# One decode step of attention and a gated feed-forward layer: q as four rows, one loop for heads 0 to 30, and the two projections summed in one row

## The chip, the cores and the metric

The kernel runs on one core of a Trainium2 chip. The metric is the device time of one execution in microseconds (us). Before the change it was 2518.3 us (median of four runs, 2518.19 to 2518.62). The names of the engines are those of the profile: PE multiplies matrices, PEld is its weight load, DVE and ACT are the vector and the scalar engine, SP issues nearly all DMA transfers.

## The reference, cut to what matters

One query token attends to a cache of 65536 positions in each of 32 heads, beside a small feed-forward layer; a gate mixes the two.

```python
# D = 512, H = 32, Sk = 65536, Dh = 128, F = 1792; all bfloat16
g = sigmoid((x * gate_w).sum(-1))
q = (x @ wq).reshape(H, Dh)
p = softmax(q @ k_cache[h].T * Dh ** -0.5)     # per head
a = concat_h(p @ v_cache[h]) @ wo
b = (silu(x @ w_gate) * (x @ w_up)) @ w_down
out = g * a + (1 - g) * b
```

k and v are 2 x 32 x 65536 x 128 x 2 bytes = 1073.7 MB. Everything else is 14 MB. Each byte is used once.

## The kernel before

Each head is cut into two chunks of 32768 positions, so there are 64 chunks. A chunk's k is one transfer of 8.39 MB and its v is another. They go in turn through a ring of three slots in SBUF, all on SP's queue. SP waits before it issues a transfer until the slot that it writes is free.

```python
WQ = KT * H * Dh
wq_sb = view(0, 0, KT, H * Dh)
dma("wq", wq_sb, ...)                            # 4.2 MB, slot 0
load("k", 0, [EK] * (KPP // EK))                 # slot 1, four pieces of 64 rows
dma("gate", gate_v, ...); dma("up", up_v, ...)   # 3.7 MB, rest of slot 0
load("v", 0, [KPP])                              # slot 2

# q as a column for each head: 32 x 4 matmuls of one column, each with its own weights
group("q_ps", [(m_x[:, h : h + 1],
    [(wq_sb[:, t, h * Dh : (h + 1) * Dh], Xc[:, t : t + 1]) for t in range(KT)])
    for h in range(H)], ...)
act("qT", qT, m_x[:, :H], ACT.Copy, ["m_x"], ["qT"])

def spread(h):                                   # q of one head into all partitions
    act("dq", dq, ident, ACT.Copy, ["ident", "qT"], ["dq"], scale=qT[:, h : h + 1])
    mms("spread", m_sp[:, :Dh], [(ones_b, dq)], ["ones_b", "dq"], ["m_sp"])
    act("q_bc", q_bc[q], m_sp[:, :Dh], ACT.Copy, ["m_sp"], [("q_bc", q)])
...
def block(n, j, m):       # DVE multiplies k by q in place; PE sums the products
...                       # gather(): DVE reduces the sums, ACT takes exp
def pv(n):                # 64 matmuls of 4 x 512: the weights times v
...
spread(0)
for n in range(N - 1):
    ...
    if n: load("k", n, [KPP]); load("v", n, [KPP])
    m = EK if n in (0, N - 2) else HK
    for j in range(0, KPP, m):
        block(n, j, m)
        ...
    gather()
    if n == 0:
        gate(); hidden()                         # frees slot 0
    ...
```

PE's instructions of heads 1 to 30 are a loop of ten turns of three heads; head 0 and head 31 are written out. In the last chunk PE also does both projections, and the last v comes in five pieces (128, 64, 32, 16 and 16 rows), so that little work is left behind the last one:

```python
row("b_ps", wd, ...)                     # m_x[0:1] = h @ w_down
act("row_b", row_b, m_x[0:1, :D], ..., scale=ngval[0:1, :])
row("a_ps", wo, ...)                     # m_sp[0:1] = o @ wo without the last head
act("row_a", row_a, m_sp[0:1, :D], ..., scale=gval[0:1, :])
for i, j in enumerate(range(0, KPP, EK)):
    if i == 2:                           # turn both rows to 4 x 128, eight matmuls in fp32
        mms("rest_ps", m_sp[:OT, :P], [... for r in (row_b, row_a) for q in range(OT)], ...)
        act("rest4", ...)
    block(n, j, EK)
    ...
column(n, V_END[:1]); sum_ps(h, H); norm(h, H); column(n, V_END[1:], V_END[0])
# then Z, l_ps, out_sb and the output's transfer
```

The softmax here doesn't subtract the row's maximum and nothing guards it: scores larger than these inputs give would overflow.

## Time and profile before

| What | Value | Read from |
|---|---|---|
| time; span of the profiled run | 2518.3 us; 2516.7 us | runs; page |
| bytes moved by DMA | 1088.04 MB | page, part 2 |
| DMA rate, 320 to 2440 us | 434 GB/s | DMA view of that window |
| first transfer issued | 1.0 us | timeline |
| last piece of v usable, output issued | 2512.1, 2514.2 us | timeline |

The lines of the page that say what bounds the kernel are the DMA rows. The first line of the fence gives busy time and share of the span of two engines; the rows after it are shares and GB/s in 40 equal slices; then comes the data queue with packets, MB and share of the 16 DMA engines' span, the queue of instruction packets, and the chain of work that ended last, by engine.

```profile
PE 1972.7 (78%) x9177; PEld 410.3 (16%) x5215; DVE 1268.4 (50%) x291; ACT 99.2 (4%) x404; POOL 1.9 (0%) x9
...
DMA  9999999999999999999999999999999999999998
GB/s 423 432 433 433 433 432 437 434 435 434 433 433 433 434 437 433 434 433 433 433 433 434 434 432 435 435 435 435 434 433 433 433 434 436 434 433 434 433 434 376
...
q1 hardware_dynamic: 20744, 1087.78, 99.8%
q8 instruction: 13, 0.21, 0.0%
...
DMA 46%; PE 40%; DVE 13%; ACT 1%; issue 0%; another core or an unknown queue 0%; SPq 0%; DVEq 0%; ACTq 0%
```

The rate is 432 to 437 GB/s in all but the first and the last slice, and 434 in the mean from 320 to 2440 us. The Trainium skill, "DMA: Bandwidth & Descriptors", section "Where 436 GB/s comes from", gives 435.2 GB/s as the ceiling of the path into SBUF, so this trace sits on it. The last line would suggest that PE is 40% of the problem. It says only that each transfer was *issued* when PE had freed its slot; it doesn't say that the queue had run out of work by then. That must be read from issue times, as in the timeline of the start. Columns: start, us, engine, line, operation, output and input, count, and idle time of the engine with what ended it.

```profile
13.21 3.57 PE L285 MATMUL m_x<-Xc,slot_65 128*128 128x1 bf16 x128 [10.62 <-DMA slot_65<-in_A_wq_dram]
18.29 4.42 DVE L344 TENSOR_TENSOR slot_66<-slot_66,q_bc_78 128x8192 bf16<-128x8192 bf16 x1 [15.50 <-ACT q_bc_78 L294]
45.11 6.86 PE L285 MATMUL m_x<-Xc,slot_65 128*128 128x1 bf16 x112 [0.35 <-ACT gval L294]
51.99 0.33 SPq L181 DMA_DIRECT2D slot_65<-in_A_k_cache_dram  x1
52.37 0.43 SPq L181 DMA_DIRECT2D slot_66<-in_A_v_cache_dram  x1
61.77 16.18 PE L257 MATMUL O_ps<-slot_67,P_sb_83 128*4 128x512 bf16 x64 [9.80 <-DMA slot_67<-in_A_v_cache_dram]
77.98 0.33 SPq L181 DMA_DIRECT2D slot_67<-in_A_k_cache_dram  x1
```

The PV matmuls of chunk 0 start when v has landed (61.8 us). By then k and v of chunk 1 have been in the queue for nearly 10 us. A transfer of 8.39 MB takes 19.3 us at this rate, so k of chunk 1 lands near 81 us and v near 100 us, and k of chunk 2 is issued at 78.0 us. The queue is never empty.

The timeline of the end shows the other edge of the stream. The first two lines are the last exp of the last chunk (ACT), the next four are PE's work on the last v.

```profile
2501.66 0.26 ACT L294 ACTIVATE P_sb_84<-S_sb_82 128x64 bf16<-128x64 f32 x1 [3.46 <-DVE S_sb_82 L369]
2501.82 0.19 ACT L294 ACTIVATION_READ_ACCUMULATOR P_sb_84<-S_sb_82 128x1 f32 x1
2502.09 3.44 PE L257 MATMUL m_c<-P_sb_84,slot_65 128*128 128x1 bf16 x127 [1.20 <-ACT P_sb_84 L294]
2508.09 0.18 PE L257 MATMUL m_c<-P_sb_84,slot_65 128*128 128x1 bf16 x1 [2.56 <-issue]
2508.56 3.12 PE L257 MATMUL m_c<-P_sb_84,slot_65 128*128 128x1 bf16 x112
2512.12 0.77 PE L257 MATMUL m_c<-P_sb_84,slot_65 128*128 128x1 bf16 x16 [0.43 <-DMA slot_65<-in_A_v_cache_dram]
...
2514.20 0.34 SPq L181 DMA_DIRECT2D out_dram<-out_sb  x1
```

PE waits at the end for the last piece of v (2512.12), and the output's transfer is issued 2.1 us later.

### The profile page before, as it was taken

The numbers are of one execution on the slowest core, as the hardware profiler recorded it, in microseconds if no ns is written. First come the engines' busy times: TensorE is split into PE (matmuls) and PEld (weight loads), VectorE is DVE, ScalarE is ACT, GpSimd is POOL, SyncE is SP. The second block draws the span as 40 slices with busy tenths as digits, with TensorE's granted clock in tenths as the row PEclk, the third lists the DMA queues.
The fourth block names the chain that finished last, engine by engine and source line by source line (L and its number), as shares of the span: only waits on it lengthen the run. The fifth ranks groups of instructions, "written<-read, shape, count | busy, mean of one in ns | idle before, by whom it ended". The sixth has DMA issues, their size and how long they took to land.

```text
span 2516.7 us, 15579 instructions
## 1 busy us (share of the span) xinstructions
PE 1972.7 (78%) x9177; PEld 410.3 (16%) x5215; DVE 1268.4 (50%) x291; ACT 99.2 (4%) x404; POOL 1.9 (0%) x9
## 2 busy tenths in 40 slices
PE   4777877877878778778787787787877877877787
PEld 1111111111111111111111111111111111111113
DVE  3455355464553554644545546446455364464554
ACT  0000000000000000000000000000000000000000
POOL 0000000000000000000000000000000000000000
PEclk8899989989889889899898899898988989989898
DMA  9999999999999999999999999999999999999998
GB/s 423 432 433 433 433 432 437 434 435 434 433 433 433 434 437 433 434 433 433 433 433 434 434 432 435 435 435 435 434 433 433 433 434 436 434 433 434 433 434 376
DMA packets 20767, 1088.04 MB, mean 432 GB/s; under 512 B 2314, under 2 KB 2444, under 8 KB 2700
## 3 DMA queue, kind: packets, MB, share of 16 engines
q1 hardware_dynamic: 20744, 1087.78, 99.8%
q8 instruction: 13, 0.21, 0.0%
q14 instruction: 6, 0.05, 0.0%
q10 hardware_dynamic: 4, 0.00, 0.0%
HBM read 1087.77 MB, written 0.00 MB: 432 GB/s over the span
## 4 chain that ended last, share of the span: by engine, by line
DMA 46%; PE 40%; DVE 13%; ACT 1%; issue 0%; another core or an unknown queue 0%; SPq 0%; DVEq 0%; ACTq 0%
PE O_ps L257 17%; DMA slot_67<-in_A_k_cache_dram 16%; DMA slot_65<-in_A_k_cache_dram 14%; DMA slot_66<-in_A_k_cache_dram 14%; PE S_ps_103 L275 11%; PE S_ps_104 L275 8%; DVE slot_66 L344 4%; DVE slot_67 L344 4%; DVE slot_65 L344 3%; DMA slot_65<-in_A_v_cache_dram 2%; DVE S_sb_82 L369 2%; PE m_c L257 1%; PE S_ps_103 L285 1%; ACT P_sb_83 L294 0%; DMA slot_65<-in_A_wq_dram 0%
## 5 line engine op out<-in xcount | busy, mean ns | idle before, releaser
L344 DVE TENSOR_TENSOR slot_67<-slot_67,q_bc_79 128x16384 bf16<-128x16384 bf16 (+1 forms) x28 | 208.2, 7469 | 146.5 <-DMA slot_67<-in_A_k_cache_dram 146.5
L369 DVE TENSOR_REDUCE S_sb_82<-S_ps_104 128x128 f32<-128x1024 f32 (+1 forms) x67 | 78.8, 1177 | 392.0 <-PE S_ps_104 L275 392.0
L344 DVE TENSOR_TENSOR slot_65<-slot_65,q_bc_78 128x16384 bf16<-128x16384 bf16 x22 | 190.2, 8689 | 146.3 <-DMA slot_65<-in_A_k_cache_dram 146.3
L344 DVE TENSOR_TENSOR slot_66<-slot_66,q_bc_78 128x16384 bf16<-128x16384 bf16 (+1 forms) x24 | 190.6, 7978 | 138.0 <-DMA slot_66<-in_A_k_cache_dram 122.5
L344 DVE TENSOR_TENSOR slot_66<-slot_66,q_bc_79 128x16384 bf16<-128x16384 bf16 x20 | 172.9, 8689 | 122.4 <-DMA slot_66<-in_A_k_cache_dram 122.4
L344 DVE TENSOR_TENSOR slot_65<-slot_65,q_bc_79 128x16384 bf16<-128x16384 bf16 x20 | 172.9, 8689 | 120.2 <-DMA slot_65<-in_A_k_cache_dram 120.2
L344 DVE TENSOR_TENSOR slot_67<-slot_67,q_bc_78 128x16384 bf16<-128x16384 bf16 x20 | 172.9, 8689 | 117.8 <-DMA slot_67<-in_A_k_cache_dram 117.8
L275 PE MATMUL S_ps_103<-slot_65,ident 128*128 128x512 bf16 x651 | 186.6, 457 | 0.0
L275 PE MATMUL S_ps_103<-slot_67,ident 128*128 128x512 bf16 x680 | 185.8, 441 | 0.0
L275 PE MATMUL S_ps_103<-slot_66,ident 128*128 128x512 bf16 x650 | 184.9, 454 | 0.0
L257 PE MATMUL O_ps<-slot_67,P_sb_83 128*4 128x512 bf16 x704 | 155.9, 383 | 28.1 <-ACT P_sb_83 L294 18.3
L257 PE MATMUL O_ps<-slot_66,P_sb_84 128*4 128x512 bf16 x704 | 153.7, 379 | 19.3 <-ACT P_sb_84 L294 19.3
L257 PE MATMUL O_ps<-slot_65,P_sb_83 128*4 128x512 bf16 x640 | 139.7, 379 | 18.3 <-ACT P_sb_83 L294 18.3
L257 PE MATMUL O_ps<-slot_67,P_sb_84 128*4 128x512 bf16 x640 | 139.7, 379 | 18.3 <-ACT P_sb_84 L294 18.3
L257 PE MATMUL O_ps<-slot_65,P_sb_84 128*4 128x512 bf16 x640 | 139.7, 379 | 18.3 <-ACT P_sb_84 L294 18.3
L257 PE MATMUL O_ps<-slot_66,P_sb_83 128*4 128x512 bf16 x640 | 139.8, 379 | 17.5 <-ACT P_sb_83 L294 17.5
L275 PE MATMUL S_ps_104<-slot_67,ident 128*128 128x512 bf16 x680 | 150.7, 379 | 0.0
L275 PE MATMUL S_ps_104<-slot_65,ident 128*128 128x512 bf16 x651 | 143.9, 379 | 0.0
L275 PE MATMUL S_ps_104<-slot_66,ident 128*128 128x512 bf16 x650 | 143.9, 379 | 0.0
L285 PE MATMUL S_ps_103<-slot_65,ident 128*128 128x512 bf16 x21 | 12.8, 608 | 134.9 <-DVE slot_65 L344 134.9
L285 PE MATMUL S_ps_103<-slot_66,ident 128*128 128x512 bf16 x22 | 13.2, 598 | 134.2 <-DVE slot_66 L344 134.2
L285 PE MATMUL S_ps_103<-slot_67,ident 128*128 128x512 bf16 x24 | 13.9, 581 | 125.0 <-DVE slot_67 L344 125.0
(99 smaller groups left out, 719.0 us busy)
## 6 DMA issues: line engine op xcount, KB each, us to landing
slot_66<-in_A_k_cache_dram SPq DMA_DIRECT2D x4, 2048.0 KB, 24.4
slot_67<-in_A_k_cache_dram SPq DMA_DIRECT2D x4, 2048.0 KB, 30.7
slot_65<-in_A_wq_dram SPq DMA_DIRECT2D x1, 4096.0 KB, 12.1
slot_66<-in_A_wo_dram SPq DMA_DIRECT2D x1, 4096.0 KB, 32.5
slot_65<-in_A_v_cache_dram SPq DMA_DIRECT2D x1, 4096.0 KB, 37.4
slot_65<-in_A_v_cache_dram SPq DMA_DIRECT2D x1, 2048.0 KB, 40.7
slot_65<-in_B_w_gate_dram SPq DMA_DIRECT2D x1, 1792.0 KB, 34.6
slot_65<-in_B_w_up_dram SPq DMA_DIRECT2D x1, 1792.0 KB, 38.3
```

The source lines that it names most:

```text
L257: ins = nc.tensor.matmul(out_ap, lhsT=a, rhs=b, start=start and i == 0, stop=stop and i == len(pairs) - 1,)
L275: ins = nc.tensor.add_instruction(mybir.InstMatmult(name=nc.get_next_instruction_name(), engine=mybir.EngineType.PE, ins=[nc.tensor.lower_ ...
L285: ins = nc.tensor.matmul(out_ap, lhsT=a, rhs=b, start=first, stop=last)
L344: "products", lambda: nc.vector.tensor_tensor(out=w, in0=w, in1=q_rep, op=ALU.mult),
L369: lambda: nc.vector.tensor_reduce(out=S_sb[b][:, :m], in_=S_ps[r][:, :m, :], axis=AXIS.X, op=ALU.add),
```

## The change

It is meant to make PE's program shorter and the constants smaller:

- q becomes four rows of 1024 (partitions 0, 32, 64 and 96), with a column of x as the stationary operand of two matmuls of 512 columns at a time: 16 weight loads and 32 matmuls instead of 128 of each. The spread of one head then contracts over one row.
- gate and up are loaded ahead of k of chunk 0, and the gate and the hidden layer are computed ahead of it. So head 0 is like the others, and PE's loop runs over heads 0 to 30: eleven turns of three heads, with an exit after the first head of the last turn.
- The two projections are summed in one row: ACT writes (1-g)*b, DVE adds g*a. Turning the row takes four fp32 matmuls instead of eight, one block later.

The diff, cut to its core:

```diff
-    load("k", 0, [EK] * (KPP // EK))
     ... gate, up ...
+    load("k", 0, [HK] * (KPP // HK))
     load("v", 0, [KPP])
@@ q
-            (m_x[:, h : h + 1],
-             [(wq_sb[:, t, h * Dh : (h + 1) * Dh], Xc[:, t : t + 1]) for t in range(KT)])
-            for h in range(H)
+            [(q_ps[32 * g : 32 * g + 1, i * W : (i + 1) * W],
+              [(x_col, wq_sb[:, t, (2 * g + i) * W : (2 * g + i + 1) * W])
+               for t, x_col in enumerate(x_cols)])
+             for i in range(2)]
+            ... for g in range(OT)
-    act("qT", qT, m_x[:, :H], ACT.Copy, ["m_x"], ["qT"])
+    for g in range(OT):
+        act("q4", q4[32 * g : 32 * g + 1, :], q_ps[32 * g : 32 * g + 1, :], ACT.Copy, ...)
@@ spread
-        act("dq", dq, ident, ACT.Copy, ["ident", "qT"], ["dq"], scale=qT[:, h : h + 1])
-        mms("spread", m_sp[:, :Dh], [(ones_b, dq)], ["ones_b", "dq"], ["m_sp"])
+        act("dq", dq, q4[32 * g : 32 * g + 1, i * Dh : (i + 1) * Dh], ACT.Copy, ...)
+        mms("spread", m_sp[:, :Dh], [(ones_b[0:1, :], dq)], ["ones_b", "dq"], ["m_sp"])
@@ start
+    gate()
+    hidden()
+    act("O_sb0", O_sb, ones[0:VB, 0:1].to_broadcast([VB, VB * Dh]), ACT.Copy, ["ones"], ["O_sb"])
     spread(0)
-        m = EK if n in (0, N - 2) else HK
+        m = EK if n == N - 2 else HK
-        if n == 0:
-            gate()
-            hidden()
@@ tail
-    row_a = O_sb[0:1, :D]
-    act("row_a", row_a, m_sp[0:1, :D], ACT.Copy, ..., scale=gval[0:1, :])
-        if i == 2:   # rest_ps: eight matmuls over (row_b, row_a)
+        if i == 3:   # rest_ps: four matmuls over row
+        if i == 1:
+            dve("row2", lambda: nc.vector.scalar_tensor_tensor(
+                out=row[:, :D], in0=m_sp[0:1, :D], scalar=gval[0:1, :], in1=row[:, :D],
+                op0=ALU.mult, op1=ALU.add), ...)
@@ PE's program
-        with nc.Fori(0, rounds, 1, engines=[PE], head_slot={PE: 0}) as r:
-            for i, o in enumerate(body[0]):
-                put(o, {s: val + r * step[i, s] for s, val in o.waits.items()})
+        with nc.Fori(0, rounds + 1, 1, engines=[PE], head_slot={PE: 0}) as r:
+            turn_of(0, r)
+            with nc.tensor.If(r < rounds):
+                for i in range(1, BODY):
+                    turn_of(i, r)
```

More of the change, by code (lines that the diff above doesn't have):

```diff
@@ L122 @@
     slot = [ring_pool.tile([P, SLOT], bf16, name=f"slot{i}") for i in range(SLOTS)]
-    x_row = sb("x_row", [1, D], bf16)
-    gw_row = sb("gw_row", [1, D], bf16)
+    row = sb("row", [1, 3 * D // 2], f32)
+    x_row, gw_row, xg = (row.bitcast(bf16)[:, i * D : (i + 1) * D] for i in range(3))
     ones = sb("ones", [P, P], f32)
@@ L130 @@
     Xc = sb("Xc", [P, KT], bf16)
-    qT = sb("qT", [P, H], f32)
-    dq = sb("dq", [P, Dh], bf16)
+    QP = H // OT
+    q4 = sb("q4", [P, QP * Dh], bf16)
+    dq = sb("dq", [1, Dh], bf16)
     q_bc = [sb(f"q_bc{i}", [P, Dh], bf16) for i in range(2)]
@@ L144 @@
     eg = sb("eg", [P, FT], f32)
-    xg = sb("xg", [1, D], bf16)
     s_t = sb("s_t", [1, 1], f32)
@@ L148 @@
     rest4 = sb("rest4", [OT, P], f32)
-    row_b = sb("row_b", [1, D], f32)
     unit = sb("unit", [1, OT * OT], f32)
@@ L269, in fn @@
             held = None
-            for out_ap, pairs in parts:
-                for i, (a, b) in enumerate(pairs):
-                    first, last = i == 0, i == len(pairs) - 1
-                    if a is held:
-                        ins = nc.tensor.add_instruction(
-                            mybir.InstMatmult(
-                                name=nc.get_next_instruction_name(), engine=mybir.EngineType.PE,
-                                ins=[nc.tensor.lower_ap(b), weights],
-                                outs=[nc.tensor.lower_ap(out_ap)],
-                                start_tensor_calc=first, stop_tensor_calc=last,
-                                tile_size=(P, P), tile_position=(0, 0), ldweights=False,
-                            )
-                        )
-                    else:
-                        ins = nc.tensor.matmul(out_ap, lhsT=a, rhs=b, start=first, stop=last)
-                        weights = ins.ins.ins[1]
-                    held = a
+            for part in parts:
+                part = part if isinstance(part, list) else [part]
+                for i in range(len(part[0][1])):
+                    for out_ap, pairs in part:
+                        a, b = pairs[i]
+                        first, last = i == 0, i == len(pairs) - 1
+                        if a is held:
+                            ins = nc.tensor.add_instruction(
+                                mybir.InstMatmult(
+                                    name=nc.get_next_instruction_name(),
+                                    engine=mybir.EngineType.PE,
+                                    ins=[nc.tensor.lower_ap(b), load.ins[1]],
+                                    outs=[nc.tensor.lower_ap(out_ap)],
+                                    start_tensor_calc=first, stop_tensor_calc=last,
+                                    tile_size=load.tile_size, tile_position=load.tile_position,
+                                    ldweights=False,
+                                )
+                            )
+                        else:
+                            ins = nc.tensor.matmul(out_ap, lhsT=a, rhs=b, start=first, stop=last)
+                            load = ins.ins
+                        held = a
             return ins
@@ L310 @@
     dve("Xc", lambda: nc.vector.tensor_copy(out=Xc, in_=m_x[:, :KT]), ["m_x"], ["Xc"])
+    q_ps = S_ps[0].rearrange("p k r -> p (k r)")
+    W = 512
+    assert QP * Dh == 2 * W
     group(
@@ L315 @@
         [
-            (
-                m_x[:, h : h + 1],
-                [(wq_sb[:, t, h * Dh : (h + 1) * Dh], Xc[:, t : t + 1]) for t in range(KT)],
-            )
-            for h in range(H)
+            [
+                (
+                    q_ps[32 * g : 32 * g + 1, i * W : (i + 1) * W],
+                    [
+                        (x_col, wq_sb[:, t, (2 * g + i) * W : (2 * g + i + 1) * W])
+                        for t, x_col in enumerate(x_cols)
+                    ],
+                )
+                for i in range(2)
+            ]
+            for x_cols in [[Xc[:, t : t + 1] for t in range(KT)]]
+            for g in range(OT)
         ],
-        units(0, 0, WQ) + ["Xc"], ["m_x"],
+        units(0, 0, WQ) + ["Xc"], [("S_ps", 0)],
     )
-    act("qT", qT, m_x[:, :H], ACT.Copy, ["m_x"], ["qT"])
+    for g in range(OT):
+        act("q4", q4[32 * g : 32 * g + 1, :], q_ps[32 * g : 32 * g + 1, :], ACT.Copy,
+            [("S_ps", 0)], [("q4", g)])
     def spread(h):
-        act("dq", dq, ident, ACT.Copy, ["ident", "qT"], ["dq"], scale=qT[:, h : h + 1])
-        mms("spread", m_sp[:, :Dh], [(ones_b, dq)], ["ones_b", "dq"], ["m_sp"])
+        g, i = divmod(h, QP)
+        act("dq", dq, q4[32 * g : 32 * g + 1, i * Dh : (i + 1) * Dh], ACT.Copy,
+            [("q4", g)], ["dq"])
+        mms("spread", m_sp[:, :Dh], [(ones_b[0:1, :], dq)], ["ones_b", "dq"], ["m_sp"])
         q = h % 2
@@ L382 @@
     P_all = [("P_sb", i, u) for i in range(2) for u in range(RS)]
-    pending = []
+    pending = [H - 1]
     def pv(n):
@@ L474, in gate, with project @@
         )
-    def row(key, w_v, names, cols, cname, ks, bank, bname):
+    EARLY = ["x_row", "gw_row", "xg"]
+    def project(key, w_v, names, cols, cname, ks, bank, bname):
         mms(key, bank[0:1, :D], [(cols[:, k : k + 1], w_v[:, k, :]) for k in ks],
@@ L570 @@
     turn_outputs(1)
-    row("b_ps", wd, units(ws, 0, WO), hT, "hT", range(FT), m_x, "m_x")
-    act("row_b", row_b, m_x[0:1, :D], ACT.Copy, ["m_x", "ngval"], ["row_b"], scale=ngval[0:1, :])
-    row("a_ps", wo, units(ws, WO, WL), M, "M", range(H), m_sp, "m_sp")
-    row_a = O_sb[0:1, :D]
-    act("row_a", row_a, m_sp[0:1, :D], ACT.Copy, ["m_sp", "gval"], ["O_sb"], scale=gval[0:1, :])
+    project("b_ps", wd, units(ws, 0, WO), hT, "hT", range(FT), m_x, "m_x")
+    act("row", row[:, :D], m_x[0:1, :D], ACT.Copy, ["m_x", "ngval"], ["row"] + EARLY,
+        scale=ngval[0:1, :])
+    project("a_ps", wo, units(ws, WO, WL), M, "M", range(H), m_sp, "m_sp")
     for i, j in enumerate(range(0, KPP, EK)):
-        if i == 2:
+        if i == 3:
             mms(
@@ L581 @@
                 [
-                    (unit[:, OT * q : OT * (q + 1)], r[:, P * q : P * (q + 1)])
-                    for r in (row_b, row_a)
+                    (unit[:, OT * q : OT * (q + 1)], row[:, P * q : P * (q + 1)])
                     for q in range(OT)
                 ],
-                ["unit", "O_sb", "row_b"], ["m_sp"],
+                ["unit", "row"], ["m_sp"],
             )
@@ L589 @@
         block(n, j, EK)
+        if i == 1:
+            dve(
+                "row2",
+                lambda: nc.vector.scalar_tensor_tensor(
+                    out=row[:, :D], in0=m_sp[0:1, :D], scalar=gval[0:1, :], in1=row[:, :D],
+                    op0=ALU.mult, op1=ALU.add,
+                ),
+                ["m_sp", "gval", "row"], ["row"],
+            )
         while len(todo) > 1:
@@ L622 @@
     rounds = (H - 2) // BODY
-    first, last = 1, 1 + rounds * BODY
+    assert H == 2 + rounds * BODY
     with tc.tile_critical():
@@ L643, in pe @@
         def pe(a, b):
-            return [o for o in plan.ops[cut[a] if a else 0 : b] if o.engine == "PE"]
-        for o in pe(0, cut[first]):
+            return [o for o in plan.ops[a:b] if o.engine == "PE"]
+        for o in pe(0, cut[0]):
             put(o, o.waits)
-        body = [pe(first + r * BODY, cut[first + (r + 1) * BODY]) for r in range(rounds)]
+        heads = [pe(cut[h], cut[h + 1]) for h in range(H - 1)]
+        body = [[heads[r * BODY + i] for i in range(BODY)] for r in range(rounds)]
@@ L649 @@
+        body.append([heads[rounds * BODY]])
         step = {}
-        for i, o in enumerate(body[0]):
-            if "POOL" in o.waits:
-                nc.tensor.wait_ge(sems["POOL"], o.waits.pop("POOL"))
-            for s, val in o.waits.items():
-                step[i, s] = body[1][i].waits[s] - val if rounds > 1 else 0
-            for r, b in enumerate(body):
-                assert b[i].key == o.key, (b[i].key, o.key)
-                assert b[i].waits == {
-                    s: val + r * step[i, s] for s, val in o.waits.items()
-                }, (r, o.key, o.waits, b[i].waits)
@@ L660 @@
-        PE = mybir.EngineType.PE
-        with nc.Fori(0, rounds, 1, engines=[PE], head_slot={PE: 0}) as r:
-            for i, o in enumerate(body[0]):
-                put(o, {s: val + r * step[i, s] for s, val in o.waits.items()})
-        for o in pe(last, len(plan.ops)):
+        for i in range(BODY):
+            for j, o in enumerate(body[0][i]):
+                if "POOL" in o.waits:
+                    nc.tensor.wait_ge(sems["POOL"], o.waits.pop("POOL"))
+                for s, val in o.waits.items():
+                    step[i, j, s] = body[1][i][j].waits[s] - val
+                for r, b in enumerate(body):
+                    if i < len(b):
+                        assert b[i][j].key == o.key, (b[i][j].key, o.key)
+                        assert b[i][j].waits == {
+                            s: val + r * step[i, j, s] for s, val in o.waits.items()
+                        }, (r, o.key, o.waits, b[i][j].waits)
@@ L665, with turn_of @@
+        def turn_of(i, r):
+            for j, o in enumerate(body[0][i]):
+                put(o, {s: val + r * step[i, j, s] for s, val in o.waits.items()})
+        PE = mybir.EngineType.PE
+        with nc.Fori(0, rounds + 1, 1, engines=[PE], head_slot={PE: 0}) as r:
[3 more added lines that the diff above has]
+                    turn_of(i, r)
+        for o in pe(cut[H - 1], len(plan.ops)):
             put(o, o.waits)
```

## The prediction

> **What bounds the kernel.** Its DMA queue. The page gives 1088 MB over 2516.7 us, the data queue busy 99.8%; between 320 and 2440 us every slice shows 432 to 435 GB/s. The Trainium skill, "DMA: Bandwidth & Descriptors", section "Where 436 GB/s comes from", puts the fabric's ceiling at 435.2 GB/s; this trace sits on it. PE (78%) and DVE (50%) have slack. The SP view of waits and the timeline show each load issued well before its turn: k of chunk 1 at 52 us, though the queue is full until v of chunk 0 lands at 61.8; later about a whole transfer (19.3 us) is still queued. Only the bytes, the work before the first transfer (1.0 us) and after the last landing (2512.1 us to the output issue at 2514.2) can move the time.
>
> **What the change does.** It changes no bytes.
>
> 1. Start. q was 128 weight loads and 128 one-column matmuls, 3.6 us (timeline, 13.2 to 16.8). Now 32 matmuls of 512 columns: at the 0.41 us (slow clock) and 0.22 us (full clock) spacing that the trace shows for this shape, 7 to 10 us, estimated. Then four ACT copies of 1x1024, some 1.2 us each (estimate from 0.68 us for 1x512). Gate and hidden now come first (PE 3 to 7 us), so the first product on DVE starts at 31 to 35 us instead of 18.3. Head 0's first half of k lands near 31.4 us, the second near 41, v at 60 to 61.5 (estimated from bytes and rate), so the PV matmuls still start near 61 us, as before at 61.8. Slot 0 is freed at 27 to 33 us instead of 52, slot 1 at about 57 instead of 52; the queue needs them at 61 and 81. Off the path. Two DMAs fewer may save 0.2 to 0.4 us [...].
>
> 2. Each head: dq is one row and the spread matmul contracts over one row; ACT is cheaper by 0.2 to 0.3 us. Off the path. The branch adds tenths of us of PE time per turn, against some 8 us of PE slack per chunk. Instruction packets: none on queue 8 between 320 and 2440 us, so the loop is not refetched; "Runtime: NRT & Kernel Launch", section "Instruction fetch mechanics", gives PE 2048 instructions; the body, about 1220, still fits.
>
> 3. Tail. The scaled a-row moves from ACT to DVE (512 elements, about 0.65 us), behind the second product, where DVE is the bound (products and reductions back to back from 2482 to 2497). It delays the last exp from 2501.7 to about 2502.3. Eight fp32 matmuls become four, where PE has slack. The column matmuls (3.4 us, an idle of 2.6 us beside an instruction packet, 3.1 us) end at 2511.7, and the last piece of v lands at 2512.1. So 0 to 0.5 us shows.
>
> **Predicted:** 2518.2 us, 8 in 10 within 2517.0 to 2519.6. Faster by over 2%: 0.005; within 2%: 0.985; slower: 0.01.
>
> **What would show it.** Right: 433 to 435 GB/s in every middle slice, first product at 31 to 35 us, PV of chunk 0 near 61, k of chunk 1 issued near 30, last v landing within 1 us of 2512. The last exp about 0.6 us later relative to the last k landing.
>
> **What would make it wrong.** A loop with an inner exit that is refetched each turn (packets on queue 8 in the middle, PE idle by "issue"); q later than estimated, so that PV of chunk 0 slips beyond 75 us and the queue runs dry; the instruction-fetch idle in the last columns falling elsewhere (up to 2.5 us either way).

## The result, and the profile after

The changed kernel took 2518.59 us (median of four fast runs, 2518.18 to 2519.18), the kernel before 2518.28 us beside it. The ratio is 1.0001, with a 95% interval of 0.9984 to 1.0018: the same.

The same lines of the page, of the changed kernel:

```profile
PE 1977.6 (79%) x9081; PEld 405.9 (16%) x5101; DVE 1268.6 (50%) x288; ACT 101.9 (4%) x404; POOL 1.9 (0%) x9
...
GB/s 423 433 433 432 432 434 433 433 434 438 434 433 433 433 433 433 435 436 435 434 434 433 433 433 433 434 433 434 438 434 433 434 433 433 433 434 435 435 434 377
...
q1 hardware_dynamic: 20456, 1087.78, 99.8%
q8 instruction: 11, 0.18, 0.0%
...
DMA 47%; PE 39%; DVE 13%; ACT 0%; issue 0%; another core or an unknown queue 0%; SPq 0%
```

The bytes of the data queue are the same, 1087.78 MB, and so is the rate. Two instruction packets are gone. The start has been rearranged, as its timeline shows:

```profile
13.42 0.58 PE L290 MATMUL S_ps_100<-slot_65,Xc 128*1 128x512 bf16 x1 [10.84 <-DMA slot_65<-in_A_wq_dram]
...
19.77 4.13 ACT L299 ACTIVATE q_75<-S_ps_100 1x1024 bf16<-1x1024 f32 x4 [16.71 <-PE S_ps_100 L278]
24.24 6.85 PE L290 MATMUL m_x<-Xc,slot_65 128*128 128x1 bf16 x112 [4.20 <-ACT gval L299]
31.12 0.33 SPq L181 DMA_DIRECT2D slot_65<-in_A_k_cache_dram  x1
33.07 8.69 DVE L363 TENSOR_TENSOR slot_66<-slot_66,q_bc_77 128x16384 bf16<-128x16384 bf16 x1 [0.60 <-DMA slot_66<-in_A_k_cache_dram]
58.94 0.33 SPq L181 DMA_DIRECT2D slot_66<-in_A_v_cache_dram  x1
61.91 15.66 PE L257 MATMUL O_ps<-slot_67,P_sb_82 128*4 128x512 bf16 x64 [2.99 <-DMA slot_67<-in_A_v_cache_dram]
77.60 0.33 SPq L181 DMA_DIRECT2D slot_67<-in_A_k_cache_dram  x1
```

The first product is 14.8 us later (33.07 against 18.29). k of chunk 1 is issued 20.9 us earlier, v of chunk 1 is issued 6.6 us later, and none of it matters: the PV matmuls of chunk 0 wait for the landing of v and start at 61.9 us, 0.1 us from where they were. At the end:

```profile
2487.38 0.73 DVE L613 SCALAR_TENSOR_TENSOR row<-m_sp,gval,row 1x512 f32<-1x512 f32 x1
...
2502.42 0.26 ACT L299 ACTIVATE P_sb_83<-S_sb_81 128x64 bf16<-128x64 f32 x1 [3.46 <-DVE S_sb_81 L388]
2502.50 3.34 PE L257 MATMUL m_c<-P_sb_83,slot_65 128*128 128x1 bf16 x128 [0.84 <-DMA slot_65<-in_A_v_cache_dram]
2508.44 3.06 PE L257 MATMUL m_c<-P_sb_83,slot_65 128*128 128x1 bf16 x108 [0.92 <-issue]
2512.14 0.59 PE L257 MATMUL m_c<-P_sb_83,slot_65 128*128 128x1 bf16 x16 [0.64 <-DMA slot_65<-in_A_v_cache_dram]
...
2514.04 0.34 SPq L181 DMA_DIRECT2D out_dram<-out_sb  x1
```

The new DVE operation took 0.73 us, and the last exp came 0.76 us later than before. PE again waits for the last piece of v, at 2512.14 against 2512.12 us.

### The profile page after: what moved, and what is told of

It reads as the page before. It is cut to its first block, busy times and chain, and to the rows that moved or that the text cites. A ratio compares the mean times of both kernels' runs of the same rounds, so it can differ in the third digit from the quotient of the medians.

```text
span 2516.5 us, 15383 instructions
## 1 busy us (share of the span) xinstructions
PE 1977.6 (79%) x9081; PEld 405.9 (16%) x5101; DVE 1268.6 (50%) x288; ACT 101.9 (4%) x404; POOL 1.9 (0%) x9
## 3 DMA queue, kind: packets, MB, share of 16 engines
q1 hardware_dynamic: 20456, 1087.78, 99.8%
## 4 chain that ended last, share of the span: by engine, by line
DMA 47%; PE 39%; DVE 13%; ACT 0%; issue 0%; another core or an unknown queue 0%; SPq 0%
PE O_ps L257 17%; DMA slot_67<-in_A_k_cache_dram 16%; DMA slot_66<-in_A_k_cache_dram 15%; DMA slot_65<-in_A_k_cache_dram 14%; PE S_ps_100 L278 11%; PE S_ps_101 L278 9%; DVE slot_67 L363 4%; DVE slot_66 L363 4%; DVE slot_65 L363 3%; DMA slot_65<-in_A_v_cache_dram 2%; DVE S_sb_81 L388 1%; PE m_c L257 1%; PE S_ps_100 L290 1%; ACT P_sb_82 L299 0%; PE S_ps_101 L290 0%
## 5 line engine op out<-in xcount | busy, mean ns | idle before, releaser
L363 DVE TENSOR_TENSOR slot_67<-slot_67,q_bc_78 128x16384 bf16<-128x16384 bf16 (+1 forms) x28 | 208.2, 7467 | 143.8 <-DMA slot_67<-in_A_k_cache_dram 143.8
L363 DVE TENSOR_TENSOR slot_65<-slot_65,q_bc_77 128x16384 bf16<-128x16384 bf16 x22 | 190.2, 8688 | 140.2 <-DMA slot_65<-in_A_k_cache_dram 140.2
L363 DVE TENSOR_TENSOR slot_66<-slot_66,q_bc_77 128x16384 bf16<-128x16384 bf16 x22 | 190.3, 8688 | 122.9 <-DMA slot_66<-in_A_k_cache_dram 122.9
L363 DVE TENSOR_TENSOR slot_65<-slot_65,q_bc_78 128x16384 bf16<-128x16384 bf16 x20 | 172.9, 8688 | 120.7 <-DMA slot_65<-in_A_k_cache_dram 120.7
L363 DVE TENSOR_TENSOR slot_66<-slot_66,q_bc_78 128x16384 bf16<-128x16384 bf16 x20 | 172.9, 8687 | 120.0 <-DMA slot_66<-in_A_k_cache_dram 120.0
L363 DVE TENSOR_TENSOR slot_67<-slot_67,q_bc_77 128x16384 bf16<-128x16384 bf16 x20 | 172.9, 8688 | 117.3 <-DMA slot_67<-in_A_k_cache_dram 117.3
L257 PE MATMUL O_ps<-slot_66,P_sb_83 128*4 128x512 bf16 x704 | 153.7, 379 | 19.3 <-ACT P_sb_83 L299 19.3
```

The lines of the kernel that those rows point to most:

```text
L257: ins = nc.tensor.matmul(out_ap, lhsT=a, rhs=b, start=start and i == 0, stop=stop and i == len(pairs) - 1,)
L363: "products", lambda: nc.vector.tensor_tensor(out=w, in0=w, in1=q_rep, op=ALU.mult),
```

## The experiments

Theory A is that of the prediction: the stream of bytes through one queue is the only bound, and all that the change moves lies in slack. The rivals are B and C: the start, or the start and the tail, are on the critical path, and what the change gains in one place it loses in another. Later comes a pair, A1 and A2, about what instruction packets cost. Each edit is made on the changed kernel. Results are medians; the kernel before ran beside each and gave 2518.3 us.

### start_late_15 and start_late_45: how much slack the start has

```diff
+    for _ in range(15):            # or 45
+        act("q4", q4[96:97, :], q_ps[96:97, :], ACT.Copy, [("S_ps", 0)], [("q4", 3)])
```

> The changed kernel with 15 more ACT copies of 1x1024 (1.03 us each in its trace) before the gate, so all of the start is about 15.5 us later. Theory A (the DMA queue is the only bound; the start has slack): v of chunk 1, issued at 58.9 us, is now issued at about 74, still before k of chunk 1 has landed (about 81), so the queue never runs dry: 2518.5 us, within 1 us. Theory B (the start is on the critical path, and the change's gains and losses there cancel): about 2534 us.

Measured: 2518.30 us, ratio 0.9999 (0.9984 to 1.0015). SP issued k and v of chunk 1 15.5 and 16.0 us later than in the changed kernel, and the time did not move. Theory B is out.

```profile
46.64 0.33 SPq L181 DMA_DIRECT2D slot<-in_A_k_cache_dram  x1
74.98 0.33 SPq L181 DMA_DIRECT2D slot<-in_A_v_cache_dram  x1
```

> The same with 45 more copies, some 46.5 us. Theory A: v of chunk 1 is issued at about 105 us where the queue would have been empty at 81, so 24 us are lost once and not regained: 2542 us, 2539 to 2546. Theory B: 2565 us. If the DMA has spare rate to catch up: less than 2535.

Measured: 2546.91 us (2545.32 to 2547.46), ratio 1.0111 (1.0096 to 1.0127), 28.6 us over the kernel before. That is between the theories' figures, nearer to A's and just outside its range. The cause is in SP's issue times of this run:

```profile
3.52 0.48 SPq L181 DMA_DIRECT2D slot<-in_A_v_cache_dram  x1
78.40 0.33 SPq L181 DMA_DIRECT2D slot<-in_A_k_cache_dram  x1
106.62 0.33 SPq L181 DMA_DIRECT2D slot<-in_A_v_cache_dram  x1
122.43 0.33 SPq L181 DMA_DIRECT2D slot<-in_A_k_cache_dram  x1
136.35 0.33 SPq L181 DMA_DIRECT2D slot<-in_A_v_cache_dram  x1
```

The expectation had thought of one empty stretch, ahead of v of chunk 1. There were two. k of chunk 1 was late too, since the gate and hidden work that frees slot 0 was delayed with the rest: v of chunk 0 had landed at 60.4 us (from the trace's completion records), and k was issued at 78.4, so 18.0 us were empty. k landed at 101.4 us and v was issued at 106.6, another 5.2 us. The two restarts then took 23.0 and 23.4 us from issue to landing, 3.7 and 4.1 us more than a transfer in a full queue (19.3). That is 30.9 us before rounding, less about 1.2 us which came back at the end (the 16 parts of the last transfer landed within 1.74 us of each other instead of 2.94; see the unrolled run below): 29.7 us, against 29.1 us for the profiled run, 2547.46 us. The lost time is not regained in the remaining 2400 us, as one expects of a stream at its ceiling.

### k_first: the order of the first loads

```diff
+    load("k", 0, [HK] * (KPP // HK))
     G0, U0 = WQ, WQ + KT * F
     ... gate, up ...
-    load("k", 0, [HK] * (KPP // HK))
```

> The changed kernel with k of chunk 0 loaded ahead of gate and up, as before the change, while the gate and hidden work stays first on PE. gate and up land near 41 us, the first product starts near 50 instead of 33, v of chunk 1 is issued near 76 instead of 59, PV of chunk 0 starts near 77 instead of 62. Theory A: no change, 2518.5 within 1 us. Theory B: about 17 us more.

Measured: 2518.23 us, ratio 0.9999 (0.9984 to 1.0015). The first product started at 49.99 us, v of chunk 1 was issued at 75.29 us and the PV matmuls of chunk 0 started at 77.1 us, as expected, and nothing came of it. SP issues v of chunk 2 at 105.52 us, against 105.79 in the changed kernel and 105.67 in the kernel before: within two chunks three quite different starts have fallen into the same rhythm, set by the landings.

### half_pv: less work of PE, the same bytes

```diff
-                for g in range(0, KPP, VB)
+                for g in range(0, KPP, 2 * VB)
```

> Wrong result on purpose: PV takes every second group of four rows, 32 matmuls a chunk instead of 64, all bytes stay. PE loses about 430 us of busy time by spacing. Theory A: no change, 2518.5 us within 1 us. If PE's share of the chain of waits (39%) were a cost: several per cent less.

Measured: 2518.13 us, ratio 0.9999 (0.9984 to 1.0014). The page of this run has PE far less busy:

```profile
PE 1548.0 (62%) x7097; PEld 237.5 (9%) x3117; DVE 1268.8 (50%) x288; ACT 101.9 (4%) x404; POOL 1.9 (0%) x9
...
GB/s 424 433 433 432 433 433 433 435 435 434 433 433 433 433 433 435 436 437 434 433 433 433 434 433 432 434 434 434 435 435 433 433 433 433 433 435 438 435 433 374
```

429.6 us of PE's work are gone, at a lower mean granted clock too (the share of its full clock that PE was given: 0.817 against 0.903), and the time is the same. The share of PE in the chain of waits was no cost. (The check against the reference passed here and in the next run, although both are wrong: it is not sensitive enough to see half of the PV terms, or stale halves of ten chunks of v.)

### half_v: the same work, fewer bytes

```diff
-            load("v", n, [KPP])
+            load("v", n, [KPP // 2] if n in range(10, 50, 4) else [KPP])
```

> Wrong result on purpose: of ten chunks, every fourth from 10, only half of v is loaded (41.9 MB less of 1088 MB), all compute stays. Theory A (time is bytes over 434 GB/s): 96.6 us less, 2422 us, 2418 to 2427. If PE (79% busy) is a bound of its own in a chunk: less gain, 2440 us or more.

Measured: 2432.28 us (2430.61 to 2439.61), ratio 0.9666 (0.9651 to 0.9681): 86 us less, where A gave 96.6; that is outside A's range (2418 to 2427), though nearer to it than to the 2440 us of a bound by PE.

```profile
q1 hardware_dynamic: 20456, 1045.83, 99.7%
```

A half load took 9.7 to 9.9 us, as its bytes say. Of the 10.2 us that are missing in the profiled run (2431.92 us), 5.9 lie in five transfers behind half loads, which took 19.8, 20.0, 20.1, 20.8 and 21.8 us instead of 19.3. The ten transfers at these places were issued only 2.6 to 3.8 us before the one ahead of them had landed, against 11.9 us or more in the middle of the changed kernel. But a short lead alone does not decide: the other five, among them the one with the shortest lead (2.6 us, issued at 746.66), landed in time, 19.3 to 19.4 us after the one ahead. The packet records show the rate falling below 420 GB/s for a microsecond or more behind nine of the ten issues (326 at 746.66 us); which of the 16 parts of a transfer that makes late, and why only five were late in the end, stays open. So A holds for the greater part. That the compute of a chunk would soon be the bound if bytes were taken out of every chunk was not tested.

### old_tail and tail_late: the end

```diff
# old_tail
+    row_a = O_sb[0:1, :D]
+    act("row_a", row_a, m_sp[0:1, :D], ACT.Copy, ["m_sp", "gval"], ["O_sb"], scale=gval[0:1, :])
-        if i == 3:
+        if i == 2:      # with eight matmuls over (row, row_a)
-        if i == 1:
-            dve("row2", ...)
# tail_late, behind row2
+            for _ in range(10):
+                dve("row3", lambda: nc.vector.scalar_tensor_tensor(out=O_sb[0:1, :D], ...), ...)
```

> The changed kernel with the tail as before: the scaled a-row on ACT in its own row, eight fp32 matmuls for the turned row, ahead of the third block. Theory A: the last exp is about 0.7 us earlier against the last landing of k, and the last v still lands after the columns are ready for it: 2518.5 within 0.5 us. Theory C (start gains about as much as the tail loses): 0.7 us less than the changed kernel, 2517.8 us.

Measured: 2518.23 us (2518.04 to 2519.07), ratio 1.0000 (0.9987 to 1.0014). The last exp started at 2501.36 us, and PE waited for the last piece of v until 2511.80 us. Theory C's gain of 0.7 us can't be told from the spread of the runs by time alone; in the trace it has no room, for PE still sat waiting 0.64 us for the last piece, as in the changed kernel.

> The changed kernel with ten more copies of the DVE operation that adds the rows (0.73 us in its trace), into a scratch row, so the DVE chain of the last chunk is 6.7 to 7.3 us later. Theory A: the columns wait for the last v until 2512.1 us, and the slack there, about 2.3 us, is used up first: 4 to 5 us more, 2522.5 to 2524 us. Theory C (no slack in the tail): 7 us more, 2525.5 us.

Measured: 2523.39 us (2522.37 to 2523.80), ratio 1.0020 (1.0005 to 1.0036), 5.1 us over the kernel before and within A's range. The profiled run, the fastest of the four at 2522.37 us, shows the last work on v without a wait:

```profile
2487.83 7.70 DVE L622 SCALAR_TENSOR_TENSOR O_sb<-m_sp,gval,row 1x512 f32<-1x512 f32 x10
...
2510.82 0.26 ACT L299 ACTIVATE P_sb<-S_sb 128x64 bf16<-128x64 f32 x1 [3.78 <-DVE S_sb L388]
...
2513.33 3.54 PE L257 MATMUL m_c<-P_sb,slot 128*128 128x1 bf16 x128
```

The exp moved by 8.4 us and the end by 4 to 5 us. The tail thus has 3 to 4 us of slack, more than the 2.3 us that was assumed. PE's idle times in the changed kernel, from the end of its last sum for the exp (2501.66 us) to the last piece of v, fit that: 0.84 + 1.19 + 0.92 + 0.64 = 3.59 us in its timeline, three waits for pieces of v and one idle beside an instruction packet. The 0.76 us of the change lie well inside.

### unrolled: what the loop is worth

```diff
-        with nc.Fori(0, rounds + 1, 1, engines=[PE], head_slot={PE: 0}) as r:
-            turn_of(0, r)
-            with nc.tensor.If(r < rounds):
-                for i in range(1, BODY):
-                    turn_of(i, r)
+        for h in range(H - 1):
+            for o in heads[h]:
+                put(o, o.waits)
```

> The changed kernel with PE's loop of heads 0 to 30 written out: the same instructions in the same order, about 12600 on PE, so some 49 instruction packets of 16 KB on queue 8 instead of 11. Theory A1 (instruction fetch is hidden and costs nothing): 2518.5 within 0.5 us. Theory A2 (each instruction packet delays one of the 16 DMA engines by its own about 1.2 us, and the last landing waits for the engine with the most of them): the engines lag unevenly, 3 more packets on each and some with more: 2521 to 2526 us, and the spread of a transfer's 16 completions, about 1.8 us in the middle of the changed kernel, grows during the run.

Measured: 2525.32 us (2525.17 to 2525.78), ratio 1.0028 (1.0014 to 1.0041), 7.0 us over the kernel before and within A2's range. The bytes of data are the same and PE's busy time is even 5 us less. What differs is the number of instruction packets; and PE waits for the last piece of v 7 us later:

```profile
q1 hardware_dynamic: 20456, 1087.78, 99.6%
q8 instruction: 55, 0.90, 0.1%
...
2519.11 0.58 PE L257 MATMUL m_c<-P_sb,slot 128*128 128x1 bf16 x16 [0.64 <-DMA slot<-in_A_v_cache_dram]
```

A transfer counts as landed when all of its 16 parts have reported. The trace's completion records give the times of these 16, so one can see how far apart they are. This table is worked out from them (us; the last two columns count from the first completion of the wq transfer):

| Kernel | instruction packets, queue 8 | spread of the 61st transfer | spread of the last | first part of the last | last part |
|---|---|---|---|---|---|
| before | 13 | 1.72 | 3.16 | 2496.19 | 2499.35 |
| changed | 11 | 1.58 | 2.94 | 2496.43 | 2499.37 |
| half_pv | 10 | 1.63 | 2.96 | 2496.23 | 2499.19 |
| unrolled | 55 | 4.42 | 10.08 | 2496.29 | 2506.37 |

The first part of the last transfer comes at the same time in all four kernels. The last part comes 7.0 us later in the unrolled one. In the unrolled run one can follow it packet by packet: after packet 1 one of the 16 completions is late by some 1.3 us, after packet 2 two are, up to about eight; packets 9 to 16 make the same number late by another 1.3 us each, and so on. At the end eight parts lie 8.5 to 10.1 us behind the first and eight lie within 1.7 us of it. So instruction packets appear to go round eight of the 16 DMA engines, and each sets its engine's share of the data back by about 1.4 us (10 us in seven rounds), for good, since the stream has no gap in which to catch up. Completions and packets carry no engine's name, so this is an inference, but two counts support it. When 53 packets had come (transfer landed at 2509.28 us), three parts lay 8.5 us and five 9.8 to 10.1 us behind, as six rounds of eight and five more give. And the packets' own times, 0.88 to 0.97 us for 16 KB, repeat with a period of eight: 931, 921, 960, 964, 949, 879, 880, 934 ns, then 931, 921, 961, 967, 949, 881, 879, 934, and so on through the run.

### few_packets: the same, the other way

```diff
-                for g in range(0, KPP, VB)                      # PV, as in half_pv
+                for g in range(0, KPP, 2 * VB)
-                [(v[:, j, :], P_sb[n % 2][:, j : j + 1]) for j in range(at, at + m)],
+                [(v[:, j, :], P_sb[n % 2][:, j : j + 1]) for j in range(at, at + m, 2)],
-                        [(wv[:, t, bass.ds(ft, P, FT)], Xc[:, t : t + 1]) for t in range(KT)],
+                        [(wv[:, t, bass.ds(ft, P, FT)], Xc[:, t : t + 1]) for t in range(1)],
```

> Wrong result on purpose: the kernel with half the PV matmuls, and also one of four terms of the hidden layer's sums and every second column matmul of the last two chunks, so that PE has about 2500 instructions fewer in its program than the changed kernel in all and some 7 instruction packets of 16 KB on queue 8 instead of 11 (the half_pv run had 10). All bytes of data stay. Theory A2 with the pattern that the completions of the unrolled run show (packets go round 8 of the 16 DMA engines, each delays one engine by about 1.3 us, so more than 8 packets hit some engine twice): the spread of the last transfer's completions is 1.6 to 2.0 us instead of 2.9 to 3.1, the last landing comes 1.2 us earlier, and the time is 2516.9 us, 2516.4 to 2517.3. Theory A1 (packets cost nothing, the unrolled run lost its 7 us elsewhere): the last landing is unmoved, 2518.0 us within 0.3.

Measured: 2516.95 us (2516.63 to 2517.41), within A2's range, ratio 0.9994 (0.9981 to 1.0008), where the kernel before ran 2518.10 to 2518.60 beside it: no overlap, but within the interval of the ratio, so the verdict by time is the same. half_pv, with ten packets and the same halved PV, took 2518.01 to 2518.24 us in another set of rounds, which points the same way; the trace is what supports a gain. The result is wrong (relative error 0.94). (The expectation overstated the instructions saved; four packets of 256 instructions are about 1000.)

```profile
q8 instruction: 7, 0.11, 0.0%
...
2511.53 0.37 PE L257 MATMUL m_c<-P_sb,slot 128*128 128x1 bf16 x8 [0.87 <-DMA slot<-in_A_v_cache_dram]
...
2513.21 0.35 SPq L181 DMA_DIRECT2D out_dram<-out_sb  x1
```

The spread of the last transfer is 2.00 us, the last piece is usable 0.6 us earlier than in the changed kernel (2511.53 against 2512.14), and 0.2 us of work is gone behind it. With seven packets going round eight engines none is hit twice, and the spread agrees with that: it does not grow between the 61st transfer and the last (2.00 us at both). The gain in the landing is about half of what was expected in the profiled run, which was the slowest of the five.

## Why the prediction was right

**The bound.** Right: the rate after is 432 to 438 GB/s in every middle slice (433 to 435 predicted), the bytes are equal, and the last v was usable at 2512.14 us (predicted within 1 us of 2512). half_pv and half_v show it by experiment: 430 us less work of PE changed nothing, 42 MB fewer bytes took 86 us away. The queue is a little less full than the prediction had it ("about a whole transfer", 19.3 us): in the middle of the changed kernel a transfer was issued at least 11.9 us before the one ahead had landed.

**The start.** Right in kind and nearly in size: first product at 33.1 us (31 to 35 predicted), slot 0 free at 31.1 (27 to 33), slot 1 free at 58.9 (about 57), PV of chunk 0 at 61.9 (near 61). That all this lies in slack was shown by start_late_15 and k_first, and the end of the slack by start_late_45. Some terms were mis-sized. The 32 matmuls of q took 6.3 us (13.42 to 19.73), not 7 to 10: the sum took them one after another, but their starts fall into four runs of eight, about 0.43 us apart within a run until 18 us, and each run begins (13.42, 14.66, 15.90, 17.14 us) before the one ahead has ended. Some starts are thus 0.04 us apart: matmuls for different rows of q overlap. The Trainium skill, "TensorE: Matmul & The Clock Gate", part 3, "The mechanism", describes such overlap for operands that use different tiles of the array; this trace agrees in that the starts of two runs lie closer than the 0.43 us within one. The four ACT copies took 1.03 us each, not 1.2. The first half of k landed at 33.1 us, not 31.4: the first instruction packet (31.0 us) fell into this transfer; where it came later, the half landed at 31.5 us (start_late_45) and 31.7 us (few_packets). Fewer DMAs at the start were to save 0.2 to 0.4 us; from the landing of wq to that of v of chunk 0 it was 48.56 us before and 48.48 after, so at most 0.1. And dq was to become 0.2 to 0.3 us cheaper; it went from 0.39 to 0.29 us.

**The loop.** Right: no packet on the instruction queue 8 between 240 and 2440 us in the changed kernel, so the body with its exit isn't fetched again. The Trainium skill, "Runtime: NRT & Kernel Launch", section "Instruction fetch mechanics", gives PE room for 2048 instructions in blocks of 256; the body of some 1220 (a turn has 1245 records of PE in the trace) would fit, and the trace agrees with that. The compare-and-branch instruction of the exit took 0.08 us in each of the ten turns that go on and 0.21 us in the last; it lies in slack in any case.

**The tail.** Right: the DVE operation took 0.73 us (0.65 predicted), the last exp came 0.76 us later, and nothing of it shows at the end. tail_late shows that the slack there is 3 to 4 us, and old_tail that going back gains nothing. One step was only roughly right: the prediction let the columns follow the last exp. The first 128 of them don't need it. They start 0.13 us after the first piece of v has landed (2501.96 us before, 2502.37 after, from the completion records), in the changed kernel while the exp still runs, and in tail_late (2509.89 us) ahead of it (2510.82). What the DVE operation delays is PE's last sum, which ended at 2501.66 us instead of 2500.89; there PE waited for v in any case.

**Not foreseen.** The prediction asked whether the loop is fetched again and where PE's idle beside a packet falls, but not what a packet costs the data. There are two fewer now (11 against 13), and no effect on the time shows. The unrolled run shows that this is not so in general. The saving that it expected of fewer loads at the start has no support in the trace before: of the four pieces of k of chunk 0 three landed 4.8 us behind the one ahead, as their bytes at 434 GB/s give, and one 6.1 us behind, the one into which the first instruction packet (18.6 us) fell.

No version of correct result that beats both kernels came out of this. What is left is about 2 us behind the last landing and 3 us of spread. To get below nine packets with a right result one would have to take three blocks of 256 instructions out of PE's program. An estimate from the table is 1.2 us, 0.05%; it was not tried.

## What to carry to other kernels

When one queue streams at its ceiling from the first microsecond to the last, ask of a change only whether it alters the bytes, the time to the first issue, the time after the last landing, or the moment at which the queue would run empty; PE's share in the chain of waits does not answer that, issue times against landings do. Slack is a number to be measured: delay the part until the time moves (here 15.5 us at the start were free and 47 us cost 28.6). And a long program written out can cost a streaming kernel DMA time, since its instruction packets delay parts of the data: the loop, which was not fetched again, saved 7 us of 2525.

## What the Trainium skill lacked or had wrong

- "DMA: Bandwidth & Descriptors", section "Where 436 GB/s comes from", says that for transfers from HBM to SBUF the HBM side binds at about 358 GB/s. Here 920 MB came from HBM at 434 GB/s in 2120 us, with one core running, so the lower figure did not bind. The rate stands at the 435 GB/s of the SBUF side; no run here tests which part of the path sets it.
- "Runtime: NRT & Kernel Launch", section "Instruction fetch mechanics", calls the crossing of a 16 KiB block mostly hidden. No page has what it costs a kernel whose DMA queue is always full: each packet made one of the 16 parts of every later transfer late by about 1.4 us, 44 packets more cost 7.0 us, and the late parts came in a round of eight. PE was also seen idle for 2.56 us (before) and 0.92 us (changed) in the tail near such a packet; the cause of that idle was not tested.
- The same section says in its tip that there is no instruction cache that benefits from spatial locality. That does not mean that a loop is fetched anew: on PE, whose larger memory the same section gives, a body of some 1220 instructions ran turn after turn without a packet on queue 8 from 240 to 2440 us.
- No page has, for transfers issued by SP, what it costs when a full queue runs dry: the two restarts in start_late_45 took 23.0 and 23.4 us from issue to landing, against 19.3 us for a transfer in a full queue.
